# GpSimd's elementwise work moves to VectorE and ScalarE in a planner-ordered attention and double-MoE kernel, and the planner's transfer costs and choice of pass change

## The chip, the cores and the metric

The kernel runs on one core of one Trainium2 chip. The metric is the device time of one launch in microseconds (us), the median of several runs. TensorE appears in the profile as PE (matmuls) and PEld (weight loads), VectorE as DVE, ScalarE as ACT, GpSimd as POOL, and SyncE, which issues the transfers, as SP.

## The reference

A recurrence over 768 steps with a 40x40 state for each of 4x8 heads, and then two feed-forward layers with different activations over its 3072 output rows:

```python
for t in range(S):
    y[:, :, t] = np.einsum('bhd,bhde->bhe', rt, state)
    Sa = np.einsum('bhde,bhe->bhd', state, at)
    state_decay = state * wt[:, :, None, :] - np.einsum('bhd,bhe->bhde', Sa, bt)
    state = state_decay + np.einsum('bhd,bhe->bhde', vt, kt)
...
h = x @ w_in                       # 3072x320 by 320x2048, float64 weights
g = h * np.cos(h)                  # second layer: h * clip(h + 3, 0, 6) / 6
return (g @ w_out).astype(np.float32)
```

## The kernel before

**Tiling.** The 768 steps are cut into 12 chunks of 64 (`NC`, `C`). For a chunk and a batch entry the functions `pA` to `pC` load and scale the inputs and form the products within the chunk, `iA` to `iE` invert the triangular matrix of the chunk (31 dependent steps `iB`, two VectorE instructions each, on the tiles `tmp` and `Tt`), and `cL` to `cXT` apply it, carry the state on (tiles `S8a`, `Tt`, `Srep`, `ST`) and write the chunk's rows, transposed, into `x1T`. The two feed-forward layers follow chunk by chunk: `mA` multiplies 512 columns' worth into the PSUM tile `h`, ScalarE and VectorE turn it into `s`, two more instructions split `s` into a high and a low half-precision part (`ghl`), and `mB` multiplies by `wout` into `acc`. Every layer has 96 such pieces, so `s` is written by 192 VectorE instructions.

**Weights.** They come as 64-bit floats. `ld_w` loads a piece as pairs of 32-bit words, `prep_w` makes 32-bit floats of it and splits them into `win` or `wout`, high and low. There are 22 pieces for each layer. The staging areas are unused parts of `wout`, and `wstat`. In `prep_w` VectorE shifts the high word left by three and puts the sign back; the top three bits of the low word `lo` are then put in. `E_LO = 1.0, 1.0` sends this last step of every piece of both layers to ScalarE (`lo` times 2^-29 into an integer) and GpSimd (an integer add).

**What sets the order.** No engine's order is written by hand. The functions call a recorder (`Plan`), which notes each instruction's engine, its cost in ns and what it depends on. An instruction called through `nc.either` is marked `ANY` (`CPY` where it is a copy), and `ALTS` says which engines may take it. `Plan.order` then runs a list scheduler forward (`forward`) and backward (`backward`) in turn, 50 passes (`PASSES`), each taking its priorities from the one ahead of it; the start times of the pass that it ends with give the order in which the program is written. Each engine then runs its own instructions in that order, and SP issues its transfers in that order.

In `forward`, `pick` hands an `ANY` instruction to GpSimd when VectorE has enough work waiting (`POOL_GAIN`). The planner models a port that VectorE and GpSimd share: while GpSimd works, VectorE takes only instructions that don't use it, and the other way about. In `rec` a transfer's `c` is the time that SP takes to issue it.

Of the kernel before, what the change touches and what calls it, by code (L numbers as in the profile page):

```python
# [12 lines left out]
U32 = mybir.dt.uint32  # L13
AF = mybir.ActivationFunctionType
ALU = mybir.AluOpType
# [25 lines left out]
W_TOP = 2.0 ** -96  # L41
E_LO = 1.0, 1.0
T_R, T_0, T_D1, T_D2, T_W0, T_W0E, T_W1, T_W1E = 78, 70, -8, -6, -59, -30, -5, 11
# [36 lines left out]

ALTS = {"ANY": ("DVE", "POOL"), "CPY": ("DVE", "ACT")}
T_SHAPE = 96.0
FULL = (128, 128)
POOL_GAIN = -0.03
OFFSET = 110
# [3 lines left out]
class Plan:  # L89
# [68 lines left out]
    def rec(self, attr, eng, name, a, kw):  # L158
# [10 lines left out]
        if name.startswith("dma"):  # L169
            sb = outs[0] if outs[0].tensor.__class__.__name__ == "Tile" and outs[0].tensor._space != DRAM else ins[0]  # L170
            c = 475.0 if sb.shape[0] in (32, 128) or ins[0].ap[0][0] == 0 else 650.0
            by = 1
# [3 lines left out]
            if name == "dma_start":  # L176
                run = _run(outs[0], ins[0])
                run = min(run, 20480)
                dma = by / run * (9 + run * 0.045) / 16
            else:  # L180
                r, w = ins[0].shape[0], by // 2 // ins[0].shape[0]
                dma = w / 128 * 204 * (1 if r >= 64 else r / 128)
                c = 1244.0 if r == 128 and w >= 1024 else 1175.0
        elif eng == "PE":
# [60 lines left out]
    def order(self):  # L245
# [22 lines left out]
        for o in reversed(ops):  # L268
# [6 lines left out]
            if moe:  # L275
                tail[i] -= o["c"] * SHARE // 100
                nxt = tail[i]
        pr = [-t for t in tail]
        for k in range(PASSES):
            start = self.forward(pr, pred, users)  # L280
            if k < PASSES - 1:
                pr = self.backward(start, pred, users)
        return sorted(range(n), key=lambda i: (start[i], i))

# [62 lines left out]
    def forward(self, pr, pred, users):  # L347
# [17 lines left out]
        def pick(e, t):  # L365

            while q[e] and q[e][0][1] in gone:
                heapq.heappop(q[e])
            if not q[e]:
                return None  # L370
            if e == 1 and port[3] > t:
                for _, i in sorted(q[1]):
                    if i not in gone and not ops[i]["port"]:
                        return i
                return None
            if e == 3:
                if port[1] > t:
                    return None
                spare = max(0, free[1] - t) + sum(ops[i]["c"] for _, i in q[1] if i not in gone and not ops[i]["port"])
                for _, i in sorted(q[3]):  # L380
                    if i in gone:
                        continue
                    o = ops[i]
                    if o["eng"] == "POOL" or o["alt"] - spare <= POOL_GAIN * o["c"]:
                        return i
                return None
            return q[e][0][1]
# [115 lines left out]
def kernel(  # L503
# [90 lines left out]

    cnt = {}
    ldq = nc.sync
# [168 lines left out]
    def prep_w(m, kind, i):  # L765
# [4 lines left out]
        else:  # L770
# [7 lines left out]
                                           op0=ALU.bitwise_and, op1=ALU.bitwise_or)  # L778
            cnt[m] = cnt.get(m, 0.0) + E_LO[m]
            if cnt[m] < 0.999:  # L780
                nc.vector.scalar_tensor_tensor(out=x.bitcast(U32), in0=lo.bitcast(U32), scalar=29, in1=x.bitcast(U32),
                                               op0=ALU.logical_shift_right, op1=ALU.bitwise_or)
            else:
                cnt[m] -= 1.0
                nc.scalar.activation(out=lo, in_=lo.bitcast(U32), func=AF.Copy, scale=2.0 ** -29)
                nc.gpsimd.tensor_tensor(out=x, in0=x, in1=lo, op=ALU.add)
        if kind == "i":
# [724 lines left out]
```

## Time and profile before

| what | before |
|---|---|
| median of 3 runs | 1166.88 us |
| lowest and highest run | 1162.44 and 1169.42 us |
| span of the profiled execution, first to last instruction | 1170.2 us |
| busy: PE | 891.6 us (76%) |
| busy: DVE | 1011.3 us (86%), 2282 instructions |
| busy: ACT | 829.1 us (71%), 1708 instructions |
| busy: POOL | 192.2 us (16%), 218 instructions |
| share of the transfer engines, mean | 70% |

For the profiled execution nothing is recorded around its span; the span is 3.3 us longer than the median of the runs. Busy times are unions: an instruction's record overlaps the next one's by some 0.06 to 0.08 us, so that two instructions of 0.68 us that follow each other start 0.60 us apart. An average over the span mixes stages: PE is nearly idle in the first 239 us and nearly full from 420 us on.

### The profile page before, as it was taken

The numbers are of one execution on the slowest core, as the hardware profiler recorded it, in microseconds if no ns is written. First come the engines' busy times: TensorE is split into PE (matmuls) and PEld (weight loads), VectorE is DVE, ScalarE is ACT, GpSimd is POOL, SyncE is SP. The second block draws the span as 40 slices with busy tenths as digits, with TensorE's granted clock in tenths as the row PEclk, the third lists the DMA queues.
The fourth block names the chain that finished last, engine by engine and source line by source line (L and its number), as shares of the span: only waits on it lengthen the run. The fifth ranks groups of instructions, "written<-read, shape, count | busy, mean of one in ns | idle before, by whom it ended". The sixth has DMA issues, their size and how long they took to land. (4 is left out here: it accounts for less than half of the span.)

```text
span 1170.2 us, 29602 instructions
## 1 busy us (share of the span) xinstructions
PE 891.6 (76%) x11378; PEld 725.8 (62%) x11378; DVE 1011.3 (86%) x2282; ACT 829.1 (71%) x1708; POOL 192.2 (16%) x218
## 2 busy tenths in 40 slices
PE   0000321367987999898998999989999889999994
PEld 0000221366776787676876878868878668788873
DVE  7799999989999999699996999979989779986552
ACT  5576798778998777796885867958768647573341
POOL 3321123222233011021010210101103004200000
PEclk9999999977998999999998999999999999999997
DMA  7989889879898758887599775787786743521010
GB/s 221 249 184 264 201 222 214 175 147 166 212 163 158 135 104 145 169 142 152 100 139 165 136 138 118 128 155 157 141 134 113 123 99 68 92 53 36 1 26 15
DMA packets 474360, 162.63 MB, mean 139 GB/s; under 512 B 446789, under 2 KB 456049, under 8 KB 473826
## 3 DMA queue, kind: packets, MB, share of 16 engines
q1 hardware_dynamic: 473922, 159.99, 69.4%
q8 instruction: 91, 1.49, 0.5%
q10 hardware_dynamic: 288, 0.67, 0.2%
q14 instruction: 59, 0.48, 0.1%
HBM read 80.09 MB, written 25.61 MB: 90 GB/s over the span
## 5 line engine op out<-in xcount | busy, mean ns | idle before, releaser
L459 PE MATMUL acc<-wout,ghl 128*128 128x320 f16 x2304 | 357.7, 303 | 5.2 <-DVE xs L459 2.7
L459 PEld LDWEIGHTS <-win 128*128 128x128 f16 x3328 | 310.6, 101 | 62.1 <-issue 13.2
L459 PEld LDWEIGHTS <-ghl 128*128 128x128 f16 x2304 | 217.1, 99 | 85.1 <-issue 4.1
L459 ACT ACTIVATE s<-h,cvec 128x512 f32<-128x512 f32 x192 | 130.7, 682 | 124.9 <-PE h L459 75.5
L459 PE MATMUL h<-x1T,win 128*128 128x256 f16 (+1 forms) x1664 | 196.1, 278 | 13.6 <-DVE s L459 8.1
L459 PE MATMUL h<-x2T,win 128*128 128x256 f16 (+1 forms) x1664 | 185.2, 266 | 3.2 <-DVE s L459 3.2
L459 DVE TENSOR_TENSOR ghl<-s,ghl 128x512 f16<-128x512 f32 x178 | 123.2, 693 | 5.8 <-ACT ghl L455 3.6
L459 PE MATMUL p<-ART,KBT 120*128 120x64 f16 x384 | 21.5, 204 | 136.6 <-DMA KBT<-KBs 77.3
L459 DVE TENSOR_TENSOR Tt<-Tt,tmp 128x126 f32<-128x126 f32 (+22 forms) x372 | 104.4, 281 | 4.3
L459 DVE TENSOR_TENSOR tmp<-Tt,Lt 128x126 f32<-128x126 f32 (+22 forms) x372 | 101.8, 274 | 7.2 <-DMA Lt<-Ls 2.6
L459 DVE SCALAR_TENSOR_TENSOR s<-h,s 128x512 f32<-128x512 f32 x96 | 65.7, 686 | 46.1 <-ACT s L459 45.5
L459 PEld LDWEIGHTS <-KBT 120*128 120x128 f16 x384 | 18.1, 104 | 140.7 <-DMA KBT<-KBs 95.5
L455 ACT ACTIVATE ghl<-s 128x512 f16<-128x512 f32 x125 | 77.8, 624 | 31.0 <-DVE s L459 26.6
L459 DVE SCALAR_TENSOR_TENSOR s<-s,h 128x512 f32<-128x512 f32 x96 | 65.0, 679 | 23.0 <-ACT s L459 22.9
L459 PE MATMUL t<-E,GF 128*128 128x40 f16 x1152 | 45.6, 183 | 42.1 <-DVE GF L459 41.0
L459 PEld LDWEIGHTS <-GF 128*128 128x128 f16 x1152 | 38.4, 98 | 48.4 <-DVE GF L459 21.1
L459 POOL TENSOR_TENSOR wout<-wout 128x512 int32<-128x512 int32 (+2 forms) x29 | 45.7, 1581 | 138.0 <-ACT wout L459 90.8
L459 PE MATMUL t<-FS,NT 128*128 128x40 f16 x768 | 36.5, 182 | 18.3 <-DVE FS L459 7.1
L459 POOL TENSOR_TENSOR wstat<-wstat 128x512 int32<-128x512 int32 (+1 forms) x16 | 30.4, 1898 | 109.7 <-ACT wstat L459 57.8
L459 PEld LDWEIGHTS <-ART 120*128 120x128 f16 (+1 forms) x704 | 43.6, 106 | 5.5 <-issue 3.0
L459 POOL TENSOR_TENSOR S8a<-S8a,xy 40x320 f32<-40x320 f32 x16 | 19.7, 1233 | 151.4 <-DVE tmp L459 78.2
L459 PEld LDWEIGHTS <-NT 128*128 128x128 f16 x768 | 32.1, 98 | 19.4 <-issue 12.2
(162 smaller groups left out, 1761.9 us busy)
## 6 DMA issues: line engine op xcount, KB each, us to landing
raw<-in_arbk_dram SPq DMA_DIRECT2D x46, 320.0 KB
v<-in_vv_dram SPq DMA_DIRECT2D x96, 80.0 KB
pip<-Dec SPq DMA_DIRECT2D x46, 160.0 KB
wout<-in_moe_w_in_dram SPq DMA_DIRECT2D x12, 512.0 KB
Ls<-LN SPq DMA_DIRECT2D x48, 128.0 KB
Lt<-Ls SPq DMA_DIRECT2D x48, 128.0 KB
TT<-Thl SPq DMA_DIRECT2D x12, 512.0 KB
wstat<-in_moe_w_out_dram SPq DMA_DIRECT2D x10, 512.0 KB
```

The source lines that it names most:

```text
L455: self.nc.scalar.activation(func=AF.Copy, **kw)
L459: getattr(getattr(self.nc, attr), name)(*a, **kw)
```

## The change

`ALTS` lets VectorE alone take what is marked `ANY`; copies still go to VectorE or ScalarE. `prep_w` puts the three low bits in with one VectorE instruction, and the ScalarE and GpSimd instructions of that step are gone. GpSimd is left with memsets. The planner's issue cost of a transfer, 475 or 650 ns before, becomes 520 to 960 ns by the number of its pieces, and that of a transposing transfer 1310 or 1390 ns in place of 1175 or 1244. `Plan.order` keeps the start times (and the choice of engine) of the pass whose last start is earliest, in place of those of the fiftieth pass.

```diff
-E_LO = 1.0, 1.0
...
-ALTS = {"ANY": ("DVE", "POOL"), "CPY": ("DVE", "ACT")}
+ALTS = {"ANY": ("DVE",), "CPY": ("DVE", "ACT")}
...
-            c = 475.0 if sb.shape[0] in (32, 128) or ins[0].ap[0][0] == 0 else 650.0
...
+                k = by // run
+                c = 520.0 if k <= 64 else 640.0 if k <= 128 else 960.0 if sb.shape[0] == 40 else 740.0
...
-                c = 1244.0 if r == 128 and w >= 1024 else 1175.0
+                c = 1390.0 if r == 128 and w >= 1024 else 1310.0
...
+        best = None
         for k in range(PASSES):
             start = self.forward(pr, pred, users)
+            if best is None or max(start) < best[0]:
+                best = max(start), start, [o["on"] for o in ops]
             if k < PASSES - 1:
                 pr = self.backward(start, pred, users)
+        _, start, on = best
+        for o, e in zip(ops, on):
+            o["on"] = e
...
-                spare = max(0, free[1] - t) + sum(ops[i]["c"] for _, i in q[1] if i not in gone and not ops[i]["port"])
-                for _, i in sorted(q[3]):
-                    if i in gone:
-                        continue
-                    o = ops[i]
-                    if o["eng"] == "POOL" or o["alt"] - spare <= POOL_GAIN * o["c"]:
-                        return i
-                return None
             return q[e][0][1]
...
-            cnt[m] = cnt.get(m, 0.0) + E_LO[m]
-            if cnt[m] < 0.999:
-                nc.vector.scalar_tensor_tensor(out=x.bitcast(U32), in0=lo.bitcast(U32), scalar=29, in1=x.bitcast(U32),
-                                               op0=ALU.logical_shift_right, op1=ALU.bitwise_or)
-            else:
-                cnt[m] -= 1.0
-                nc.scalar.activation(out=lo, in_=lo.bitcast(U32), func=AF.Copy, scale=2.0 ** -29)
-                nc.gpsimd.tensor_tensor(out=x, in0=x, in1=lo, op=ALU.add)
+            nc.vector.scalar_tensor_tensor(out=x.bitcast(U32), in0=lo.bitcast(U32), scalar=29, in1=x.bitcast(U32),
+                                           op0=ALU.logical_shift_right, op1=ALU.bitwise_or)
```

The planner's numbers decide the order on every engine, so the order has to be read from the built programs. Three places show what moves.

**First place.** VectorE near the start of the program, where it works on the first layer's first weight pieces (in `wstat` and `wout_70`, on the way to `win_68`); the decays of the first four chunks (`win_69`) are just ahead. Before:

```order
L459 SCALAR_TENSOR_TENSOR wstat<-wstat 128x512
L459 TENSOR_SCALAR wout_70<-wout_70 128x512 x2
L459 SCALAR_TENSOR_TENSOR wout_70<-wout_70 128x512 x2
L459 TENSOR_SCALAR wout_70<-wout_70 64x512
L459 SCALAR_TENSOR_TENSOR wout_70<-wout_70 64x512
L459 CAST win_68<-wstat 128x512
L459 SCALAR_TENSOR_TENSOR FS_82<-v_136,FS_82 128x8x40
L459 TENSOR_TENSOR win_68<-wstat,win_68 128x512
```

The same place in the changed program:

```order
L456 SCALAR_TENSOR_TENSOR wstat<-wstat 128x512
L456 TENSOR_SCALAR wout_70<-wout_70 128x512
L456 SCALAR_TENSOR_TENSOR wstat<-wstat 128x512
L456 SCALAR_TENSOR_TENSOR wout_70<-wout_70 128x512
L456 TENSOR_SCALAR wout_70<-wout_70 128x512
L456 SCALAR_TENSOR_TENSOR wout_70<-wout_70 128x512 x2
L456 TENSOR_SCALAR wout_70<-wout_70 64x512
L456 SCALAR_TENSOR_TENSOR wout_70<-wout_70 128x512
L456 SCALAR_TENSOR_TENSOR wout_70<-wout_70 64x512
L456 TENSOR_TENSOR win_68<-wstat,win_68 128x512
L456 SCALAR_TENSOR_TENSOR wout_70<-wout_70 64x512
L456 SCALAR_TENSOR_TENSOR FS_82<-v_136,FS_82 128x8x40
```

Each piece now has two of the three-operand instructions on VectorE where it had one, and its step on GpSimd is gone.

**Second place.** The middle of the program, where the state of each chunk is carried on. Before, on GpSimd (`Tt` and `S8a` hold the state, `xy` the chunk's rows and the state's increment, `ARs` and `ghl` parts of other steps):

```order
L459 TENSOR_TENSOR Tt<-S8a,Tt 40x8x40
L459 TENSOR_TENSOR S8a<-S8a,pd_142 40x320
L459 TENSOR_TENSOR ARs_79<-raw_116,ARs_79 128x8x40
L459 TENSOR_TENSOR ghl_150<-s_147,ghl_150 128x512
L459 TENSOR_TENSOR S8a<-S8a,pd_142 40x320
L459 TENSOR_TENSOR S8a<-S8a,xy_144 40x320
L459 TENSOR_TENSOR Tt<-S8a,Tt 40x8x40
```

In the changed program GpSimd has only the memsets of `Tt` there, and such instructions stand on VectorE, between the steps of the inversion (`tmp`, `Tt`):

```order
L456 SCALAR_TENSOR_TENSOR xy_144<-t_139,cvec,pd_142 104x320
L456 TENSOR_TENSOR Tt<-Tt,tmp 128x9x14
L456 CAST S8a<-xy_144 64x320
L456 TENSOR_TENSOR tmp<-Tt,Lt_92 128x130
L456 TENSOR_TENSOR S8a<-xy_144,S8a 64x320
L456 TENSOR_TENSOR Tt<-Tt,tmp 128x10x13
L456 TENSOR_TENSOR KBs_77<-raw_116,KBs_77 128x8x40
L456 TENSOR_TENSOR tmp<-Tt,Lt_92 128x120
L456 TENSOR_TENSOR S8a<-S8a,pd_142 40x320
L456 TENSOR_TENSOR Tt<-Tt,tmp 128x10x12
```

Over the program 88 such instructions pass from GpSimd to VectorE.

**Third place.** SP, just ahead of the last of the four transposes that complete the first chunk's `x1T` (after which the first layer's last rows of that chunk can start). Before:

```order
L459 DMA wstat<-in_moe_w_in_dram 128x1024
L459 DMA Ds<-raw_116 32x320
L459 DMA v_136<-in_vv_dram 64x320 x2
L459 DMA TT<-Thl_108 128x2048
L459 DMA pd_142<-Dec_98 64x16x40
L459 DMA_TRANSPOSE ST_87<-Tt 128x16x48
L459 DMA Srep_89<-Tt 40x16x40
L459 DMA wout_71<-in_moe_w_in_dram 64x1024
L459 DMA Srep_89<-Tt 40x16x40
L459 DMA_TRANSPOSE x1T_95<-S8a 128x6x64
```

The changed program there:

```order
L456 DMA wstat<-in_moe_w_out_dram 128x1024
L456 DMA pip_80<-Dec_98 64x8x80
L456 DMA Lt_92<-Tm_106 64x1024
L456 DMA_TRANSPOSE KBT_125<-KBs_77 128x8x128
L456 DMA TT<-Thl_108 128x2048
L456 DMA pd_142<-Ds 40x640
L456 DMA pd_142<-Dec_98 64x16x40
L456 DMA_TRANSPOSE ART_129<-ARs_79 128x8x128
L456 DMA Ls_103<-LN_135 64x16x32
L456 DMA_TRANSPOSE x1T_95<-S8a 128x6x64
```

The weight loads of the second layer (`wout_71`) now stand behind the transpose; with the rest of the move 160 entries stand ahead of it on SP in place of 183, and 21 weight loads in place of 30.

## Rows read from the trace of the kernel before

**Rows 1.** Windows: stretch, length, busy (count) of PE, PEld, DVE, ACT, POOL, PEclk, DMA.

```profile
0.00:50.00 50.00, 0.00 (x0) 0.00 (x0) 35.31 (x54) 29.57 (x49) 17.10 (x36) 1.00 0.83 235
...
420.00:1035.00 615.00, 579.61 (x7401) 469.07 (x7398) 552.24 (x1312) 451.10 (x941) 84.60 (x107) 0.98 0.72 129
1035.00:1170.00 135.00, 119.08 (x1181) 95.36 (x1179) 73.13 (x156) 50.05 (x108) 0.00 (x0) 0.95 0.12 24
...
0.00:420.00 420.00, 192.92 (x2804) 161.35 (x2804) 385.91 (x816) 327.99 (x661) 107.63 (x111) 0.95 0.86 191
```

**Rows 2.** Timeline of VectorE at two places: start, duration, instruction.

```profile
420.20 0.68 DVE L459 SCALAR_TENSOR_TENSOR s<-s,h 128x512 f32<-128x512 f32 x1
...
1035.26 0.67 DVE L459 SCALAR_TENSOR_TENSOR s<-s,h 128x512 f32<-128x512 f32 x1
```

**Rows 3.** GpSimd by instruction and shape: count, busy, mean ns, idle before.

```profile
L459 POOL TENSOR_TENSOR wout<-wout 128x512 int32<-128x512 int32 x22 | 34.5, 1573 | 115.4 <-ACT wout L459 75.2 <-DVE tmp L459 12.9 <-ACT win L455 10.7
L459 POOL TENSOR_TENSOR wstat<-wstat 128x512 int32<-128x512 int32 x14 | 26.9, 1920 | 96.1 <-ACT wstat L459 55.5 <-DVE wout L459 17.2 <-DVE tmp L459 7.1
L459 POOL TENSOR_TENSOR Tt<-S8a,Tt 40x320 f16<-40x320 f32 x21 | 22.3, 1061 | 129.8 <-ACT Tt L455 72.7 <-DVE Tt L459 42.3 <-DMA pd<-Ds 10.6
L459 POOL TENSOR_TENSOR S8a<-S8a,xy 40x320 f32<-40x320 f32 x16 | 19.7, 1233 | 151.4 <-DVE tmp L459 78.2 <-DVE xy L459 72.8
```

**Rows 4.** VectorE by tile: ns min/median/max, first and last start in us, shape.

```profile
L459 DVE TENSOR_TENSOR NT<-LN,NT x47: 686/687/2011, 60.5 to 933.9; 64x512 f16<-64x512 f32 x47
...
L459 DVE TENSOR_TENSOR Tt<-S8a,Tt x23: 484/489/1466, 183.1 to 924.4; 40x320 f16<-40x320 f32 x23
...
L459 DVE TENSOR_SCALAR wout<-wout x28: 400/414/1579, 25.2 to 320.9; 128x512 int32<-128x512 int32 x22, 64x512 int32<-64x512 int32 x6
L459 DVE SCALAR_TENSOR_TENSOR wout<-wout x28: 656/680/1656, 25.9 to 323.6; 128x512 int32<-128x512 int32 x22, 64x512 int32<-64x512 int32 x6
...
L459 DVE SCALAR_TENSOR_TENSOR FS<-v,FS x48: 473/481/1566, 30.6 to 1041.8; 128x320 f16<-128x320 f32 x48
L459 DVE SCALAR_TENSOR_TENSOR FS<-t,FS x48: 471/475/483, 143.7 to 1050.6; 64x320 f16<-64x320 f32 x48
...
L459 DVE SCALAR_TENSOR_TENSOR S8a<-t,uh x48: 469/476/484, 65.0 to 1045.5; 64x320 f16<-64x320 f32 x48
```

**Rows 5.** Timelines of VectorE and of GpSimd, 25 to 34 us.

```profile
25.91 1.28 DVE L459 SCALAR_TENSOR_TENSOR wout<-wout 128x512 int32<-128x512 int32 x2
27.12 1.51 DVE L459 TENSOR_SCALAR wout<-wout 64x512 int32<-64x512 int32 x1
28.66 1.66 DVE L459 SCALAR_TENSOR_TENSOR wout<-wout 64x512 int32<-64x512 int32 x1
...
26.67 1.68 POOL L459 TENSOR_TENSOR wstat<-wstat 128x512 int32<-128x512 int32 x1 [17.25 <-DVE wout L459]
28.31 5.58 POOL L459 TENSOR_TENSOR wout<-wout 128x512 int32<-128x512 int32 x3
```

**Rows 6.** ScalarE's converting step by shape, and VectorE's waits from 0 to 420 us.

```profile
L459 ACT ACTIVATE wout<-wout 128x512 int32<-128x512 uint32 x22 | 14.5, 665 | 0.1
...
DVE wstat L459 <- ACT wstat L459: 6.0, 2, 5.7
...
DVE s L459 <- ACT s L459: 5.0, 4, 3.7
```

**Rows 7.** TensorE's waits, 420 to 1035 us: total us, times, longest.

```profile
PE h L459 <- DVE s L459: 9.4, 8, 2.2
...
PE t L459 <- DVE GF L459: 3.7, 6, 1.4
PE t L459 <- DVE S8a L459: 3.5, 5, 1.9
```

**Rows 8.** Timeline of SP, 226 to 230 us: two issues.

```profile
226.95 1.21 SPq L459 DMA_TRANSPOSE x1T<-S8a  x1
...
229.48 0.85 SPq L459 DMA_DIRECT2D Srep<-Tt  x1
```

More of the change, by code (lines that the diff above doesn't have):

```diff
@@ L78, in tile @@
         return t
-ALTS = {"ANY": ("DVE", "POOL"), "CPY": ("DVE", "ACT")}
+ALTS = {"ANY": ("DVE",), "CPY": ("DVE", "ACT")}
 T_SHAPE = 96.0
 FULL = (128, 128)
-POOL_GAIN = -0.03
 OFFSET = 110
@@ L593, in dp @@
         return nc.either
-    cnt = {}
     ldq = nc.sync
```

## The prediction

> **What bounds the kernel now.** I read the windows first [rows 1], because the averages of the page hide three stages. From the start to 420 us VectorE is the full engine: 385.9 us busy of 420, while TensorE has 192.9. Of VectorE's 34.1 us of idle time 14.7 us lie in the first 50 us. From 420 to 1035 us TensorE is busy for 579.6 of 615 us, VectorE for 552.2: both are nearly full, TensorE more so. After 1035 us VectorE has 73.1 us of work in 135 us, and TensorE (119.1 us, nearly all of what is left until its last matmul) sets the pace. So work on VectorE counts in full in the first stage, partly in the second, hardly in the third. The two boundaries are instructions that both programs have: the 9th and the 73rd VectorE instruction that makes `s` of the second feed-forward layer, at 420.20 and 1035.26 us [rows 2]. In the order, TensorE's matmuls ahead of these two are nearly the same before and after, so what is won or lost at them is passed on.
>
> **What leaves GpSimd, and what VectorE pays.** GpSimd runs 132 elementwise instructions: 44 integer adds of the weight preparation (1573 and 1920 ns each in the two big groups) and 88 of the `ANY` kind, such as the 21 on `Tt` at 1061 ns and the 16 on `S8a` at 1233 ns [rows 3]. Each of the 44 becomes one three-operand instruction on VectorE, a form that is there: the median is 680 ns [rows 4], and two in a row take 1.28 us from 25.91 us on, with the next one starting at 27.12 [rows 5], so one costs 0.605 us of VectorE. 44 of them cost 26.5 us, all in the first stage. The 88 others cost 0.40 to 0.60 us each by the same measure (a 40x320 one has a median of 489 ns [rows 4]); their sum is 45.5 us. Copies that change engine between VectorE and ScalarE take 3 us off; in all VectorE's own work grows by 69 us.
>
> Where it falls I counted in the order, with these durations. Ahead of the 420 us boundary: 26.5 us for the adds, 7 us for moved instructions and copies, and 9 us less because 31 steps of the next chunk's inversion now stand behind the boundary. That is +24.7 us. Ahead of the 1035 us boundary it is +58.5 us, since 20 reductions of the final tests (12 us) pass into the last stage. There they lie under TensorE's 119.1 us, beside 73.1 us of VectorE's [rows 1]; without that cover they would cost their 12 us. The middle so gets 58.5 - 24.7 = 33.8 us.
>
> **What VectorE gets back.** The trace shows VectorE held up while GpSimd works. At 27.12 us a 64x512 shift takes 1.51 us, and at 28.66 us its three-operand partner 1.66 us, while GpSimd runs adds from 26.67 and from 28.31 us [rows 5]; the medians of the two forms are 0.41 and 0.68 us [rows 4]. Groups that read two SBUF tiles have a maximum two to three times their median: 2011 against 687 ns, 1466 against 489, 1566 against 481. Groups that read PSUM have none: 475 and 483, 476 and 484 [rows 4]. I set each VectorE instruction that overlaps a GpSimd elementwise one against the median of its kind without such overlap: 34.2 us are lost in the first stage (183 instructions), 18.2 us in the middle (187), 52 us in all. As a check, the 817 instructions ahead of the first boundary cost 350 us at undisturbed spacing, and 350 + 34.2 is within 2 us of the 385.9 us busy. With GpSimd down to memsets I take all of it as given back. The bounds are half of it, if some of the long ones have another cause, and all.
>
> VectorE's balance by then is: first stage +24.7 - 34.2 = -9.5 us; middle +33.8 - 18.2 = +15.6 us.
>
> A rule speaks against the change: the Trainium skill (Perfetto Trace Analysis, Optimizing Scalar/DVE Operations) says that with a saturated VectorE it may make sense to offload work to ScalarE or even GpSimd, and this change goes the other way on an engine that is 86% busy. The same paragraph adds that the two share a read port, so that moving work between them might not help; rows 4 and 5 agree with this half. By the rule's first half alone the first stage would cost +24.7 us, by the rows it gives 9.5 back.
>
> **What ScalarE gets back.** 44 converting instructions of 665 ns go [rows 6], some 25 us of ScalarE before 420 us, where it has 328 us of work [rows 1]. VectorE waits there on ScalarE for `wstat` (6.0 us) and for `s` (5.0 us) [rows 6]. The long one of these (5.7 us) falls in the first 50 us; behind it the new order has weight work for VectorE to do. I take 2 us off VectorE's idle time; the bounds are 0 and the 11 us of these two rows.
>
> **The middle.** TensorE's 579.6 us of 615 stay; VectorE would come to 552.2 + 15.6 = 567.8 us, still under it. So the pace stays with TensorE, and what I price is its 35.4 us of idle time. 16.6 us of it are waits that end in VectorE [rows 7]. VectorE's load rises from 0.898 to 0.923; if waits for it go as load over idle share, they grow by 0.36 of 16.6, or 6 us. Against it, a link of the state's chain on GpSimd took 1061 and 1233 ns and takes 489 on VectorE [rows 3, 4], which I put at -3 us. I take +3; the bounds are 0 (TensorE hides it all) and +15.6 (VectorE sets the pace).
>
> **The planner's numbers.** The issue costs move towards the trace: a transpose took SP 1.21 us and a 40-partition store 0.85 us [rows 8], where the planner had 1.175 and 0.65 and now has 1.31 and 0.96. What this does I can read only from the order: fewer weight loads stand ahead of the first chunk's last transpose. The better pass is better by the planner's own count. I price both at nothing, with the middle's idle time as their bound (rivals).
>
> **The sum.** 1170.2 - 9.5 - 2 + 3 = 1161.7 us for the profiled execution. Its span is 3.3 us over the median, so 1158.4 us for the median: I say 1158, 0.7% faster.
>
> **The rivals.**
> 1. *The plan fits better, and the middle closes up.* TensorE's idle time there falls from 35 to 20 us, and the granted clock, 0.98 [rows 1], which stands for 12 us lost to half speed, gives 5 us back: 1158.4 - 3 - 15 - 5 = 1135 us. For it: half of the idle time is on VectorE, and GpSimd's durations, up to twice the undisturbed ones, are no longer in the plan. Against: a fuller VectorE.
> 2. *VectorE sets the pace in the middle.* Then the 15.6 us come in full and eat the gain: 1170.2 - 11.5 + 15.6 - 3.3 = 1171 us. For it: 92% load. Against: TensorE has more to do.
> 3. *Slower: VectorE sets the pace, and TensorE's clock pays.* Each of TensorE's gaps costs more than its length when the clock falls after it: 35.4 us of idle time stand beside 12 us of clock. In that ratio 15.6 us become 21, or, with a few more instructions late because the state's chain now queues behind the inversion on VectorE, 25: 1176 to 1180 us. It decides from the point where the middle grows by 17 us (11.5 gained, and 5.8 to be seen as slower).
> 4. *VectorE gets nothing back*: its long instructions were long for another reason. The first stage then grows by 24.7 - 2 and the middle by up to 33.8: 1189 to 1223 us. Against it are the PSUM groups, which were never long. Beside it stands the first half of the rule of the Trainium skill named above.
> That the change does nothing is excluded by the order: the 132 instructions are gone from GpSimd.
>
> **How the numbers follow.** 0.5% is about what a measurement of this kernel can tell from no change: 1161.0 to 1172.7 us is "the same". The forecast gets 0.46 (its own range 1150 to 1166 us, by the bounds of ScalarE's and the middle's terms; 0.32 of it under 1161), rival 1 0.21, rival 2 0.17 (0.12 within 0.5%), rival 3 0.13, rival 4 0.03. Faster: 0.32 + 0.21 = 0.53. Same: 0.14 + 0.12 = 0.26. Slower is the rest, 0.21. The range 1137 to 1178 us leaves out part of rivals 1 and 3, and 4, about 2 in 10.
>
> **What the changed profile would show.** GpSimd's busy time falls to what its memsets take, about 20 us. VectorE has 130 instructions more, its `NT` and `Tt` groups have maxima near their medians, and its busy time is about 1011 + 69 - 52 = 1028 us. ScalarE's count falls by 42 and its busy time by 25 us. The 9th `s` of the second layer starts near 409 us and the 73rd near 1027 us; TensorE's idle time between them is near 38 us. The prediction is wrong if VectorE's two-input instructions stay long, if the 9th `s` doesn't come earlier (then something else, such as the transfers with a share of 0.86, paced the first stage), or if the stretch from the 9th to the 73rd changes by more than some 6 us.

## The result and the profile after

The changed kernel takes 1175.85 us (median of 8 runs, 1171.67 to 1177.10) against 1167.26 us (8 runs, 1162.44 to 1169.68) of the kernel before in the same comparison: ratio 1.0068, interval 1.0048 to 1.0089. It is 0.7% slower, where 0.7% faster was forecast.

The profiled execution has a span of 1175.3 us. Its page, busy times by engine:

```profile
PE 893.2 (76%) x11378; PEld 725.7 (62%) x11378; DVE 1017.7 (87%) x2412; ACT 809.5 (69%) x1666; POOL 20.8 (2%) x86
```

GpSimd is down to its memsets, VectorE has the 130 instructions more, and its busy time has risen by only 6.4 us, where 17 (69 - 52) were forecast. ScalarE, though the title names it, took over none of GpSimd's work: it has 42 instructions fewer. Three views say how that came. First the windows, to set beside [rows 1], with the same columns:

```profile
420.00:1035.00 615.00, 575.27 (x7320) 465.47 (x7318) 556.20 (x1389) 448.30 (x935) 7.43 (x35) 0.97 0.70 129
1035.00:1170.00 135.00, 122.57 (x1208) 97.91 (x1205) 85.07 (x177) 54.32 (x118) 0.00 (x0) 0.96 0.13 26
0.00:420.00 420.00, 195.38 (x2854) 162.36 (x2855) 376.43 (x849) 306.86 (x615) 13.37 (x51) 0.93 0.86 189
```

In the first 420 us VectorE is busy 376.43 us where it was 385.91: 9.5 us less, the number that the prediction worked out. But its idle time is 43.6 us where it was 34.1, and the two boundary instructions stand almost where they stood (timeline of VectorE, beside [rows 2]):

```profile
418.73 0.69 DVE L456 SCALAR_TENSOR_TENSOR s<-s,h 128x512 f32<-128x512 f32 x1
...
1038.23 0.69 DVE L456 SCALAR_TENSOR_TENSOR s<-s,h 128x512 f32<-128x512 f32 x1
```

So the first stage gained 1.5 us, the middle went from 615.1 to 619.5 us, and the last stage from 135.0 to 137.1. Second, VectorE's groups by tile (ns min/median/max), beside [rows 4]:

```profile
L456 DVE TENSOR_TENSOR NT<-LN,NT x48: 686/687/690, 64.5 to 1004.1; 64x512 f16<-64x512 f32 x48
L456 DVE TENSOR_TENSOR Tt<-S8a,Tt x44: 484/489/492, 165.0 to 1005.5; 40x320 f16<-40x320 f32 x44
L456 DVE SCALAR_TENSOR_TENSOR FS<-v,FS x48: 473/482/494, 32.1 to 1044.7; 128x320 f16<-128x320 f32 x48
```

Every long instruction is gone: the maxima of 2011, 1466 and 1566 ns are now 690, 492 and 494. Third, TensorE's waits in the middle (419 to 1038 us), beside [rows 7]:

```profile
PE t L456 <- DMA FT<-FS: 11.2, 5, 4.3
PE h L456 <- DVE s L456: 8.3, 8, 2.1
PE q L456 <- DMA Lt<-Tm: 7.3, 6, 2.3
...
PE t L456 <- DVE GF L456: 2.2, 3, 1.6
...
PE t L456 <- DVE S8a L456: 0.6, 1, 0.6
```

The waits that end in VectorE sum to 17.4 us over all rows of the view (16.9 before); those that end in a transfer to 19.8 (15.1 before), 11.2 of them for the transposed `FT`.

### The profile page after: what moved, and what is told of

The parts are those of the page before. It is cut to its first block, busy times and chain, and to the rows that moved or that the text cites. A ratio compares the mean times of both kernels' runs of the same rounds, so it can differ in the third digit from the quotient of the medians.

```text
span 1175.3 us, 29423 instructions
## 1 busy us (share of the span) xinstructions
PE 893.2 (76%) x11378; PEld 725.7 (62%) x11378; DVE 1017.7 (87%) x2412; ACT 809.5 (69%) x1666; POOL 20.8 (2%) x86
## 4 chain that ended last, share of the span: by engine, by line
DVE 40%; PE 31%; DMA 12%; issue 6%; ACT 6%; SPq 4%; DVEq 0%; ACTq 0%
PE h L456 12%; PE acc L456 11%; DVE Tt L456 5%; PE t L456 4%; DVE tmp L456 4%; SPq L456 4%; DVE s L456 3%; DVE ghl L456 3%; DVE S8a L456 3%; DVE wout L456 3%; DVE win L456 2%; PE q L456 2%; DVE raw L456 2%; DMA pip<-Dec 2%; DMA out_dram<-s 2%
## 5 line engine op out<-in xcount | busy, mean ns | idle before, releaser
L456 DVE TENSOR_TENSOR ghl<-s,ghl 128x512 f16<-128x512 f32 x192 | 131.4, 684 | 4.8 <-ACT ghl L452 2.7
L456 DVE TENSOR_TENSOR tmp<-Tt,Lt 128x126 f32<-128x126 f32 (+22 forms) x372 | 91.8, 247 | 15.2 <-DMA Lt<-Ls 11.8
L452 ACT ACTIVATE ghl<-s 128x512 f16<-128x512 f32 x135 | 83.9, 624 | 20.2 <-DVE s L456 14.8
L456 DVE TENSOR_TENSOR Tt<-Tt,tmp 128x126 f32<-128x126 f32 (+22 forms) x372 | 91.5, 246 | 3.3
L456 PE MATMUL q<-Lt,Tt 32*32 32x32 f32 x768 | 31.5, 199 | 21.9 <-DMA Lt<-Tm 21.9
L456 PEld LDWEIGHTS q<-Lt,Tt 32*32 32x32 f32 x768 | 28.8, 115 | 26.1 <-DMA Lt<-Tm 24.3
L456 PEld LDWEIGHTS <-TT 64*128 64x128 f16 (+1 forms) x768 | 26.9, 96 | 23.2 <-issue 15.7
```

What stands on the lines that cost most here:

```text
L452: self.nc.scalar.activation(func=AF.Copy, **kw)
L456: getattr(getattr(self.nc, attr), name)(*a, **kw)
```

## The experiments

Each kernel was timed in five rounds against the kernel before on the same chip. Stages are those of the prediction: to the 9th `s` of layer 2, on to the 73rd, and to the end. "PE<-DVE" and "PE<-DMA" sum TensorE's waits in the middle that end in VectorE and in a transfer, over all rows of the view of waits. The theories in the expectations are numbered through the whole series: 1 says that a new order is a draw, 2 that VectorE sets the pace wherever it is fuller, 5 that TensorE sets the pace of the middle. "Rival 3" and "rival 4" there are the better pass and the new issue costs as causes, not the prediction's rivals.

| kernel | ratio and interval | first, middle, last stage (us) | VectorE busy in the middle | PE<-DVE, PE<-DMA |
|---|---|---|---|---|
| before | 1 | 420.2, 615.1, 135.0 | 552.2 | 16.9, 15.1 |
| after | 1.0068 (1.0048 to 1.0089) | 418.7, 619.5, 137.1 | 560.2 | 17.4, 19.8 |
| inplace | 1.0150 (1.0113 to 1.0187) | 419.1, 631.3, 134.7 | 572.6 | 32.4, 10.5 |
| adds_inplace | 0.9967 (0.9943 to 0.9991) | 415.3, 615.0, 136.4 | 551.4 | 17.2, 13.7 |
| any_inplace | 1.0238 (1.0202 to 1.0273) | 421.1, 634.9, 135.8 | 573.2 | 32.5, 13.0 |
| dose_vector | 1.0091 (1.0059 to 1.0123) | 419.1, 620.0, 134.8 | 569.7 | 25.0, 8.8 |
| dose_scalar | 1.0035 (1.0013 to 1.0056) | 419.1, 616.4, 135.6 | | |
| dose_tensor | 1.0044 (1.0021 to 1.0066) | 418.1, 616.4, 135.5 | | |
| relief | 1.0020 (1.0000 to 1.0040) | 417.9, 613.5, 137.2 | 537.2 | 18.4, 14.3 |
| before_late | 1.0057 (1.0035 to 1.0080) | 419.8, 614.2, 144.3 | 527.4 | 19.2, 13.5 |
| inplace_late | 1.0172 (1.0134 to 1.0209) | 418.2, 627.5, 144.5 | 549.3 | 27.7, 11.3 |
| adds_late | 1.0024 (0.9994 to 1.0054) | 415.2, 613.8, 144.9 | | |
| inplace_gf | 1.0152 (1.0107 to 1.0198) | 415.3, 632.5, 136.4 | 572.6 | 32.8, 10.1 |
| after_first | 1.0045 (1.0016 to 1.0075) | 420.6, 617.2, 138.6 | 560.8 | 14.2, 19.9 |
| move_replan | 1.0074 (1.0045 to 1.0103) | 419.4, 621.2, 136.0 | 553.7 | 25.6, 11.5 |
| move_cost | 1.0098 (1.0059 to 1.0137) | 425.9, 612.4, 137.9 | | |
| move_best | 1.0086 (1.0052 to 1.0121) | 429.6, 612.1, 138.5 | | |
| best_only | 1.0101 (1.0067 to 1.0136) | 425.0, 612.3, 135.2 | | |
| cost_only | 1.0007 (0.9986 to 1.0027) | 433.8, 594.8, 138.0 | | |
| pass49 | 0.9982 (0.9957 to 1.0006) | 424.6, 603.7, 136.1 | | |

The stages come from one profiled execution each, whose span lies up to 10.7 us under the median of the runs (best_only: 1172.5 against 1183.23). Five kernels whose order up to the first boundary is that of before, but for a few doubled or later instructions, read 418.1 to 420.2 there (the doses, before_late, before). In the middle the spread is wider: inplace, any_inplace and inplace_late, in whose orders VectorE's work from the 9th to the 65th `s` is the same, read 552.6, 555.8 and 557.7 us there. So a stage's difference under 2 us, or 5 in the middle, says little; which kernel is faster is told by the ratio. The groups of runs were timed on different chips, each beside the kernel before.

**The move and the planner taken apart.** The order of before, kept word for word, with the 132 instructions on VectorE:

```diff
         for attr, name, a, kw in o["calls"]:
+            if kw.get("scale") == 2.0 ** -29:
+                continue
+            if attr == "gpsimd" and name == "tensor_tensor":
+                self.nc.vector.scalar_tensor_tensor(out=kw["out"].bitcast(U32), in0=kw["in1"].bitcast(U32), scalar=29,
+                                                    in1=kw["out"].bitcast(U32), op0=ALU.logical_shift_right,
+                                                    op1=ALU.bitwise_or)
+                continue
+            if o["eng"] == "ANY":
+                attr = "vector"
+                getattr(getattr(self.nc, attr), name)(*a, **kw)
+                continue
```

> The order of the kernel before is kept word for word; only where GpSimd's 132 elementwise instructions stand, VectorE runs them, and the 44 converting instructions of ScalarE are left out. Theory 1 (the move itself wins, the new order loses it): ratio 0.985 to 0.995, the 9th s of the second layer at 405 to 412 us in place of 420. Theory 2 (the move itself loses, since VectorE sets the pace wherever it is fuller): ratio 1.003 to 1.012, the 9th s not earlier than 420 us.

Measured: 1.0150, above both ranges, so theory 1 is out and theory 2 put the loss too low. The loss is in the middle (631.3 us). The first stage is 1.1 us shorter.

The move planned anew, with the old issue costs and the fiftieth pass (in the changed kernel the lines on `best` are taken out, and `c = 475.0 ... else 650.0` is back), and the two planner edits alone on the kernel before:

> The move to VectorE alone, ordered anew by the planner, with the old issue costs and the fiftieth pass. Theory 1: the order is drawn anew, ratio anywhere from 0.990 to 1.007, and not the ratio of the run with the order kept. Theory 2: 1.003 to 1.012, as with the order kept.

> The kernel before with the pass whose last start is earliest, nothing else. Theory 1 (what the planner counts and what the chip does differ by more than the passes do): ratio 0.994 to 1.008, either sign. Rival 3 (the best pass is better on the chip too): 0.985 to 0.995.

> The kernel before with the new issue costs, nothing else. Theory 1: ratio 0.994 to 1.008, either sign. Rival 4 (the new costs are what makes the order worse, since they hold transfers back on SP): 1.005 to 1.012, with the first chunk's scaled inputs later than 43.7 us.

A loss as large as the changed kernel's is there with the move alone (1.0074). Alone on the kernel before, the better pass loses (1.0101, more than any of its expectations allowed) and the new costs change nothing (1.0007). Two more complete the square: the move with the new costs but the fiftieth pass, and with the best pass but the old costs.

> The changed kernel with the fiftieth pass in place of the best. Theory 1 (passes are draws): 1.002 to 1.010, either side of the changed kernel's 1.007. If the best pass is a cost on the chip, as in the run with it alone (1.010): 0.995 to 1.002.

> The changed kernel with the old issue costs. Theory 1: 1.002 to 1.010. If the new issue costs help (alone they gave 1.0007): over 1.010.

1.0098 and 1.0086, both in theory 1's range, and with intervals that overlap those of move_replan and of the changed kernel. As a control, one pass fewer on the kernel before (`PASSES = 49`):

> The kernel before with the planner stopped one pass earlier, all else the same: a control of how far one draw of the planner's order lies from the next on the chip. Theory (orders of neighbouring passes scatter by about as much as the runs best_only, cost_only, move_best and move_cost did): anything from 0.994 to 1.010. Rival (an order that the planner thinks better is better on the chip): the ratio follows its own estimate and stays within 0.998 to 1.002.

0.9982, within both ranges. Four plans of the kernel before lie between 0.998 and 1.010 and four plans with the move between 1.0068 and 1.0098: the planner edits cannot be told from one draw of the order to the next. That the move itself loses rests on inplace, whose order is that of before, and which was planned for another split of the work. For orders planned with the move, four out of four lose, but the worst plan without it (1.0101) loses as much: how much of the changed kernel's 0.68% is the move and how much the draw, these runs don't tell.

**Which load the middle takes.** On the kernel before, in the middle alone: 29 `ghl` subtractions issued twice on VectorE, 32 `s` activations twice on ScalarE, 24 accumulation groups of `h` twice on TensorE; and 67 `ghl` casts taken off VectorE to ScalarE, in place. The first of them as a diff, without the two lines that set `mid` (`mid` picks pieces of the middle):

```diff
                 getattr(getattr(self.nc, attr), name)(*a, **kw)
+                if mid and attr == "vector" and name == "tensor_tensor" and g[4] in (1, 5):
+                    self.nc.vector.tensor_tensor(*a, **kw)
```

> The kernel before, order kept, with 29 subtractions of ghl in the middle run twice (same result): 17.4 us more of VectorE's work between 420 and 1035 us. Theory 2 (VectorE sets the middle's pace): the middle grows by 13 to 18 us, ratio 1.011 to 1.016. Theory 5 (TensorE sets it, and the run with the order kept lost for another reason): by 0 to 5 us, ratio 1.000 to 1.004.

> The kernel before, order kept, with 32 of the activations that make s in the middle run twice: 18 us more of ScalarE's work there. Theory 2: ScalarE (451 of 615 us) has room, so less than the VectorE dose: ratio 1.000 to 1.008. If any added work on the way from h to ghl costs its length, whatever the engine: 1.011 to 1.016.

> The kernel before, order kept, with 24 accumulation groups of h in the middle run twice (same result): 21 us more of TensorE's work there. Theory 2: TensorE has 35 us of idle time there, the middle grows by 5 to 12 us, ratio 1.004 to 1.010. Theory 5: by 18 to 24 us, ratio 1.015 to 1.020. If both set the pace in turn, both doses come in nearly full.

> The kernel before, order kept, with the 67 casts of ghl that VectorE had run by ScalarE at the same places: some 30 us less on VectorE (about half of it ahead of 1035 us), 37 us more on ScalarE. Theory 2: ratio 0.985 to 0.995, faster than both kernels. Theory 5: 0.998 to 1.006.

17.4 us more on VectorE cost 0.91%, or 10.6 us (4.9 of them seen in the profiled middle), between the two ranges; 18 us more on ScalarE 4.1 us; TensorE's busy time there grew by only 10 us (579.6 to 589.4) of the 21 meant, which cost 5.1 us. With 15 us less on VectorE there (27 in all) the kernel is no faster, but relief also put 35 us more on ScalarE, which at the price of the ScalarE dose is some 8 us: what the relief alone is worth it doesn't tell. By the intervals no engine's work counts one for one in these places. VectorE's 0.6 us for one and TensorE's 0.5 can't be told apart; ScalarE's is 0.2.

**The two kinds of moved work.** The diff of inplace with only the first two of its three branches (the 44 adds), and with only the third (the 88 `ANY`):

> The kernel before, order kept; only the 44 adds of the weight preparation move to VectorE (26.5 us more work there, the 44 converting instructions of ScalarE left out), the 88 others stay on GpSimd. Theory 2: what the adds had cost VectorE by holding it up comes back and about covers them, and the middle is left alone: ratio 0.997 to 1.004. If the adds are what loses: 1.008 to 1.015.

> The kernel before, order kept; only the 88 other instructions move to VectorE (45 us more work there, nearly all in the middle), the 44 adds stay on GpSimd. Theory 2: 18 us come back in the middle, some 20 us net stay, at the 0.6 us per us of the VectorE dose: ratio 1.009 to 1.015, all of it between the 9th and the 73rd s. If the adds are what loses: 0.998 to 1.004.

The two kinds have opposite signs: adds_inplace lies a little below theory 2's range, any_inplace well above it. Windows of adds_inplace, and two of its groups on VectorE by tile (the shifts, and the three-operand step that was there before):

```profile
0.00:415.00 415.00, 190.34 (x2808) 159.89 (x2809) 379.64 (x860) 306.70 (x617) 38.04 (x67) 0.95 0.88 193
415.00:1030.00 615.00, 580.45 (x7395) 469.67 (x7395) 551.43 (x1312) 451.01 (x941) 84.47 (x107) 0.98 0.73 129
...
L466 DVE TENSOR_SCALAR wout<-wout x28: 400/416/427, 25.4 to 316.5; 128x512 int32<-128x512 int32 x22, 64x512 int32<-64x512 int32 x6
L466 DVE SCALAR_TENSOR_TENSOR wout<-wout x28: 658/682/693, 26.1 to 319.3; 128x512 int32<-128x512 int32 x22, 64x512 int32<-64x512 int32 x6
```

VectorE has 44 instructions more ahead of the boundary and is busy 6.2 us less (379.9 up to the 9th `s`, 386.1 before), since its shifts no longer stretch to 1579 ns nor its other steps to 1656 [rows 4]. The stage is 4.9 us shorter, the middle as it was, and the kernel faster than both of this case. ScalarE's 44 converting instructions are gone here too; but VectorE's waits that end in ScalarE, up to the 9th `s`, are no shorter (19.6 us, 17.9 before), so it isn't ScalarE's relief that shows. Windows of any_inplace, and TensorE's waits in its middle:

```profile
0.00:421.00 421.00, 189.45 (x2813) 159.00 (x2814) 389.57 (x832) 330.04 (x661) 90.01 (x95) 0.96 0.86 190
421.00:1056.00 635.00, 583.79 (x7400) 471.48 (x7396) 573.23 (x1385) 451.68 (x941) 8.00 (x35) 0.97 0.70 125
...
PE t L462 <- DVE GF L455: 13.2, 9, 3.7
PE h L462 <- DVE s L462: 6.9, 7, 1.6
PE t L462 <- DVE S8a L462: 6.1, 7, 1.9
...
PE acc L462 <- DVE xs L462: 3.3, 4, 1.4
```

VectorE has 21 us more work in the middle and 3.5 ahead of it. The middle is 19.8 us longer, and the ratio says 27.9 us in all. What grew is TensorE's waiting for VectorE: 32.5 us in place of 16.9, above all for `GF` (13.2, was 3.7) and `S8a` (6.1, was 3.5) [rows 7].

**What of the 88 costs it.** In the middle the dose of 17.4 us cost 4.9, the 21 us of the 88 cost 19.8 (by the ratios 0.6 us for one and 1.1 us for one): it is not the sum of the load alone. Over half of inplace's 16 us falls between the 65th and the 73rd `s` (78.6 against 68.6 us), where VectorE's 44 reductions for the final tests (`acc<-win`, `acc<-wout`) stand, and of these the changed kernel passes 20 to the last stage. Three kernels issue them behind the 73rd `s`, two after each `ghl` subtraction; the order is otherwise that of before, of inplace, and of adds_inplace:

```diff
-        for i in self.order():
-            self.emit(i)
...
+        late = [i for i in l if ops[i]["grp"][0][0] == "wmax"]
...
+        cut = at[s[72]]
...
+        for i in l:
+            if i in moved:
+                continue
             self.emit(i)
+            for u in after.get(i, ()):
+                self.emit(u)
```

> The kernel before with nothing moved between engines; only the 44 wmax reductions on VectorE (and what consumes their flag) are issued later, behind the 73rd s of layer 2, two after each ghl subtraction. Theory (VectorE paces the end of the middle stretch, and the reductions stand in it): the stretch from the 65th to the 73rd s, 68 us before, falls towards the 58 to 60 us that it is when those 40 reductions are not in it, the last stage grows by less than it loses, ratio 0.994 to 1.000. Rival (TensorE is full in that stretch, so that nothing can close up): the 73rd s stays within 3 us of 1035, ratio 0.999 to 1.004, above 1 if the last stage has to make room.

> The run inplace (order of before, all 132 GpSimd operations on VectorE, 1.015) with the wmax reductions issued behind the 73rd s. Theory: half of what inplace lost in the middle was in its last interval, where the added work and the reductions stand together; the interval falls from 78 to about 66 us, ratio 1.003 to 1.008. Rival (a steady load of VectorE, alike in all chunks): the interval loses no more than the 2 us of an average chunk, ratio 1.011 to 1.018.

> The run adds_inplace (44 adds from GpSimd to VectorE, 0.9967) with the wmax reductions issued behind the 73rd s. Theory: both gains stand in different stages and add up, ratio 0.988 to 0.996, faster than both kernels. Rival (TensorE full in the end of the middle): no more than adds_inplace alone, 0.996 to 0.999.

My theory fell in all three: 1.0057, 1.0172 and 1.0024. The middle gives back 0.9, 3.8 and 1.2 us, and the last stage grows by 8 to 10 us. Window and TensorE's waits of before_late's last stage, where the kernel before has no such wait:

```profile
1034.00:1178.00 144.00, 121.15 (x1181) 96.03 (x1178) 97.69 (x199) 49.55 (x107) 0.00 (x0) 0.94 0.11 23
...
PE t L459 <- DVE GF L459: 3.0, 2, 2.1
PE p L459 <- DVE acc L459: 1.2, 1, 1.2
PE t L459 <- DVE xy L459: 0.9, 1, 0.9
PE h L459 <- DVE s L459: 0.7, 1, 0.7
```

In the order of before the reductions were free where they stood: without them the interval falls by 0.9 us. Beside the moved work they weren't: in inplace_late it falls from 78.6 to 69.8 us, near the theory's 66, but the stretch ahead of it reads 5.1 us longer, which is within the spread named above. Windows from the 65th to the 73rd `s` of before, inplace and inplace_late:

```profile
967.00:1035.00 68.00, 67.38 (x821) 54.69 (x820) 65.71 (x141) 42.57 (x89) 23.36 (x21) 1.00 0.41 75
```

```profile
972.00:1050.00 78.00, 70.45 (x829) 56.44 (x827) 75.55 (x161) 42.70 (x89) 0.00 (x0) 0.98 0.38 66
```

```profile
976.00:1046.00 70.00, 67.55 (x823) 55.04 (x822) 51.35 (x120) 42.45 (x89) 0.00 (x0) 1.00 0.41 74
```

This interval is a stage of its own. Before, both engines are full in it, TensorE for 67.4 and VectorE for 65.7 of 68 us. Then 10 us more on VectorE make it 10 us longer, one for one, and 24 us less (before_late) bring nothing. Of the dose's 17.4 us only 0.7 fell into it, which is part of why the dose was cheap.

Ahead of it, from the 9th to the 65th `s` (546.5 us before, VectorE busy for 486.0), the 88 put some 11 us more on VectorE, and the stretch is 6.1, 9.3 and 11.2 us longer (inplace, any_inplace, inplace_late); dose_vector put 16.7 us there and cost 4.3. The same amount costs more as these instructions than as doubled subtractions. Whether that comes from where they stand in VectorE's queue or from what waits for them is not shown. inplace_late doesn't tell either: in it VectorE has 3 us less to do over the whole middle than before, and the middle is 12.5 us longer, but that sum is 12 us more where VectorE's work costs and 15 us less where it was free.

`GF` being the largest wait, the next kernel issues 20 of the 88, each of which stands up to 12 VectorE instructions ahead of a `GF<-gm,GF` that doesn't need it, right behind that subtraction; the rest is inplace:

```diff
+            for m in dv[max(0, k - 12):k]:
+                if m in gone or ops[m]["on"] != "POOL" or ops[m]["eng"] != "ANY":
+                    continue
+                if any(m in ops[u]["deps"] for u in l[at[m] + 1:at[g] + 1]):
+                    continue
+                gone.add(m)
+                behind.setdefault(g, []).append(m)
```

> The run inplace (1.015, 9th to 73rd s 631 us against 615) with one difference in its order: where one of the 88 moved instructions stands up to 12 VectorE instructions ahead of a GF<-gm,GF subtraction and nothing between needs it, it is issued right behind that subtraction (20 of the 88). VectorE's work is the same. Theory (the moved instructions cost by making GF late, for which TensorE waits 13.0 us there against 3.7 before): TensorE's waits for GF fall to 4 to 8 us, the stretch from the 9th to the 73rd s to 622 to 627 us, ratio 1.006 to 1.012. Rival (VectorE's load sets the pace, wherever the instructions stand): the stretch stays at 629 to 633 us, ratio 1.012 to 1.018.

This fell too, and the rival's figures came: 1.0152, middle 632.5 us. The waits for `GF` shrank from inplace's 13.0 us, those for `S8a` and `s` grew from 7.2 and 6.2 (TensorE's waits, 415 to 1048 us):

```profile
PE t L470 <- DVE GF L463: 9.7, 9, 2.1
PE t L470 <- DVE S8a L470: 7.8, 6, 2.6
PE h L470 <- DVE s L470: 7.7, 8, 2.2
```

**The idle time at the start.** In the changed kernel SP issues three weight loads ahead of the first chunk's decay rows (`pip<-Dec`); timeline of SP:

```profile
30.15 7.23 SPq L456 DMA_DIRECT2D wout<-in_moe_w_in_dram  x3
37.47 0.65 SPq L456 DMA_DIRECT2D pip<-Dec  x1
```

Before, `pip<-Dec` was issued at 34.90 us. In after_first the loads, and what rests on them, stand behind the first two chunks' decay rows and their scaling:

```diff
+        loads = [i for i in l[:first] if ops[i]["grp"][0][0] == "ld_w" and ops[i]["grp"][0][3] in (4, 5, 6)]
...
+            if at[i] == first:
+                for u in loads:
+                    self.emit(u)
+            if at[i] == last:
+                for u in tail:
+                    self.emit(u)
```

> The changed kernel with one place of its order put back towards that of before: SP issues the three weight loads that stand ahead of the first chunks' decay rows (30.15 to 37.4 us) behind those two short transfers, and what rests on the loads (the conversions of these three pieces, one further load) is written behind the scaling of the first two chunks. Theory (VectorE's added idle time in the first 60 us is handed on to the end of the first stage): the first product of raw and pip starts near 44 us in place of 49.8, VectorE is busy 2 to 4 us more before 60 us, the 9th s of layer 2 starts at 414 to 417 us in place of 419, ratio to the kernel before 1.003 to 1.007 (the changed kernel 1.0068). Rival (the first stage ends where it does because of what is late after 200 us): the 9th s stays at 418 to 420 us, ratio 1.005 to 1.010.

The first product of `raw` and `pip` does start at 46.09 us in place of 49.76, but VectorE's busy time up to 60 us is the same (window 0 to 60, of after_first and of after):

```profile
0.00:60.00 60.00, 0.00 (x0) 0.10 (x1) 41.36 (x73) 29.45 (x52) 8.39 (x31) 1.00 0.87 220
```

```profile
0.00:60.00 60.00, 0.00 (x0) 0.10 (x1) 41.35 (x73) 29.44 (x52) 8.41 (x31) 1.00 0.88 219
```

VectorE's idle time there has only changed its place, and the 9th `s` comes at 420.6 us. The ratio of 1.0045 lies in the theory's range, and by its interval in the rival's too; the stage is the rival's.

## Why the prediction was wrong

**Right: the count and the refund.** VectorE's busy time ahead of 420 us fell by 9.5 us as worked out (up to the 9th `s` itself by 10.9), its long instructions are gone, and so rival 4 is out. For the middle the same sum came out too high: VectorE's load there grew by 8 us, not 15.6. What the Trainium skill (Perfetto Trace Analysis, Optimizing Scalar/DVE Operations) says of the shared read port agrees with this: 2011 ns became 690. On the rule's other half the runs decide by kind of work: taking the 44 adds off GpSimd gains (0.9967), taking the 88 off it loses (1.0238).

**Failed: "first stage -9.5 us".** The step took VectorE's busy time for time of the stage. 9 us of it were inversion steps that pass behind the boundary. They were taken as saved in the first stage, where VectorE was held to be the limit, and came back in the middle, where TensorE was held to hide them: the same work was counted once as a gain and hardly as a cost. Five orders of the moved program have VectorE busy for 383, 385, 375, 383 and 388 us ahead of the 9th `s` (inplace, move_replan, after, move_cost, move_best), and reach it at 419.1, 419.4, 418.7, 425.9 and 429.6 us. So VectorE's busy time by itself does not set the boundary. From inplace to the changed kernel VectorE's busy time falls by another 8 us, the boundary comes 0.4 us earlier, and idle time takes the place of the work. What the deferral does by itself no run isolates, since the rest of the order differs too.

The added 9.5 us of idle time lie all along the stage: 3.5 us before 50 us, 1.9 from there to 239 us, 4.0 behind. By what ends them, up to the 9th `s`, VectorE's waits for ScalarE grew from 17.9 to 25.2 us and those for TensorE from 0.7 to 3.7. Those that end in a transfer directly did not grow (7.3 to 6.6). But the transfers, which the prediction named as the other possible pacemaker, come in through ScalarE: the longest of VectorE's waits for it, 8.14 us, follows a wait of ScalarE's for a weight load of 8.72 us (6.08 before; timeline of ScalarE, after):

```profile
42.15 0.66 ACT L456 ACTIVATE wstat<-wstat 128x512 f32<-128x512 f32 x1 [8.72 <-DMA wstat<-in_moe_w_in_dram]
```

Where the rest of the idle time comes from is open.

Without the deferral the term is 24.7 + 9 - 34.2 = -0.5 us, and -2.9 us of busy time and -1.1 us of the stage are what inplace shows. Within that, the adds give 4.9 us, and with the 88 beside them 3.8 us are lost again (415.3 to 419.1); but inplace_gf, with the same work, reads 415.4, so that this loss is uncertain.

**Failed as a general step: "the pace stays with TensorE".** In the order of before, the 88 put 21 us more on VectorE in the middle and cost 19.8: VectorE's work came nearly in full, as in rival 2. The formula of load over idle share would have TensorE's waits for VectorE grow by some 9 us there (0.898 to 0.932); they grew by 15.6. The step took the average of 615 us for one stage. In its last eight `s` VectorE was as full as TensorE, and there the added work came one for one; that is shown by inplace against before and inplace_late. Of the rest it is open which of the 88 cost it, and whether by their place or by what waits for them; the turn of `GF` alone doesn't explain it.

**Right in size, partly by luck: the middle's +3.** The changed kernel's own order has 619.5 us there, +4.4, for half of the forecast load. Its waits for VectorE are at 17.4 us, as before, as TensorE-hides-it would have it. What grew are the waits for transfers, from 15.1 to 19.8 us. move_replan shows that planning anew took back most of inplace's loss in the middle (621.2 against 631.3): its order leaves VectorE 553.7 us of work there against 572.6. Which part of the new order does it is not shown.

**Mis-sized: the last stage at nothing.** It grew by 2.1 us. I had put 20 reductions there under TensorE's cover; before_late shows that with all 44 the stage is 9 us longer: `GF`, `acc`, `xy` and `s` come late (5.8 us) in a stage in which TensorE waited for nothing before. That they are the cause in the changed kernel is likely, but at 2 us it is not shown.

**The sum again.** Forecast span 1161.7, profiled 1175.3: 13.6 us, of which the first stage is 10.0, the last 2.1, the middle 1.4. The other 3.8 us between 1158.4 and 1175.85 are the step from span to median: this span lies 0.5 us under its median, not 3.3 above it. Rival 1 is out, since TensorE's waits in the middle rose from 35 to 39 us. Rival 3's time (1176 to 1180 us) is the nearest, but not its mechanism: the clock of the middle is 0.97 against 0.98, and the state's chain (`S8a`, 0.6 us of TensorE's waits) was not late in the changed kernel.

**ScalarE.** Its busy time fell by 19.6 us, not 25, and the credit of 2 us did not come. VectorE's waits for ScalarE on `wstat`, 6.0 us before [rows 6], rose to 10.3 (VectorE's waits, 0 to 420 us, of after), and the longest from 5.7 to 8.14 us (timeline of VectorE, after):

```profile
DVE wstat L456 <- ACT wstat L456: 10.3, 4, 8.1
```

```profile
42.93 0.43 DVE L456 TENSOR_SCALAR wstat<-wstat 128x512 int32<-128x512 int32 x1 [8.14 <-ACT wstat L456]
```

## What to carry to other kernels

Judge a move from one engine to another by the kind of work and the stage it stands in, each by itself: the same edit held a part that gained (adds beside a full VectorE, where the other engine stretched its neighbours) and a part that lost more (88 instructions that had run beside VectorE and now stand in its queue). Cut the stages by which engines are full: an average of 90% hid eight pieces in which both engines were full, and there added work came one for one. A planner that passes work behind a boundary has saved nothing there until the wait that ends last has moved; count such work in both stages. Before crediting an order to a planner's rule, time a few neighbouring orders: here they lay up to 1.2% apart.

## What the runs showed of the hardware

In this kernel GpSimd's hold on VectorE was large enough to make extra work pay: 44 instructions more (26.5 us by the prediction's count) and VectorE was busy 6.2 us less, so some 33 us came back from the disturbance of 44 adds alone. From 239 to 335 us TensorE's granted clock, a mean of times at full and at half speed, was 0.75 in the changed kernel and 0.86 before, with 58.0 us of work against 75.7. The first `s` of the first layer had come 29 us earlier (210 against 239 us), but TensorE then waited for VectorE (after, 239 to 420 us; 1.9 us before):

```profile
PE h L456 <- DVE s L456: 25.2, 5, 9.9
```

The early start came with gaps and with a lower clock; that the gaps alone lowered it was not tried.
